# A gated recurrence with a gated causal convolution: one hand-ordered plan exchanged for another, with two chunks' input products moved to GpSimd

## The chip, the cores and the metric

The kernel runs on one core of a Trainium2 chip. Times are device microseconds (us) of one execution; the time of a kernel is the median of several executions. The core has five engines that work side by side and wait for each other through semaphores: TensorE (PE; its weight loads are shown as PEld), VectorE (DVE), ScalarE (ACT), GpSimd (POOL) and SyncE (SP), which here only issues transfers. A letter q behind an engine's name (ACTq, SPq) is its queue as the issuer of a DMA.

## The reference

The inputs x, r_gate and i_gate are 4 x 6336 x 256 in fp32, that is 25,344 tokens of 256 channels. A linear recurrence runs over the tokens of each of the four sequences, and a gated unit with a causal convolution of five taps follows.

```python
a_base = sigmoid(a_param)
a_t    = exp(8.0 * sigmoid(r_gate) * log(clip(a_base, 1e-6, 1 - 1e-6)))
x_g    = sqrt(max(1 - a_t * a_t, 1e-6)) * sigmoid(i_gate) * x
h      = a_t[:, t] * h + x_g[:, t]          # for each t; y[:, t] = h
gate   = sigmoid(sum over k of conv_w[k] * y[t - 4 + k])
out    = (gate * (y @ w_val)) @ w_out
```

## The kernel before

The tokens are cut into 27 chunks (CHUNKS): one of 512, 23 of 1024, then 512, 512 and 256. Work on the output side is cut further into parts of 512 tokens (a chunk c has parts c.0 and c.1), and the 256 channels are two halves h of 128. Inputs come token-major (tokens on the partitions); the scan needs channels on the partitions, so TensorE transposes in between.

The order of all work is written out by hand in a string, PLAN (lines 33 to 118). Each word is an operation with its chunk, its half or part, and the PSUM bank that it writes (-1 for none). The loop at line 466 runs through the words and calls the function of that name, so each engine's queue holds its operations in the plan's order, and an engine that waits holds up all that is behind it. The operations, in the order in which a chunk passes through them:

| word | engine, line | what it does |
|---|---|---|
| ldri, ldx | SP, L220, L224 | load r_gate and i_gate of a chunk, and its x; 1 MB each for 1024 tokens |
| tanh | ACT, L290 | tanh of half of both gates (sigmoid from tanh), to bf16 in place |
| srT, exp | PE L295, ACT L304 | transpose the r gate, then a_t = exp(...) into aring |
| e | POOL, L310 | a_t squared into ering |
| s1, u | POOL, L318, L345 | i gate + 1, then times x: uring |
| xc, ux | PE L327, DVE L335 | for chunks in X_PE, in place of s1 and u: x is copied into PSUM by an identity matmul, two 128-token blocks at a time, and VectorE makes (gate + 1) times x from there |
| sq | ACT, L354 | square root of 1 - a_t squared, for up to three chunks at once; needs another activation table, so a table load (L472) before and after |
| nT, xg | PE L367, DVE L374 | transpose the root back, multiply it into uring |
| xgT, scan | PE L382, DVE L395 | transpose the gated input, then the recurrence of one half |
| conv, tg | PE L407, ACT L417 | convolution of a part as matmuls with diagonal weights, then tanh |
| val, gv | PE L425, DVE L430 | y @ w_val, then the gating product |
| out, osbD or osbA | PE L439, DVE L454 or ACT L450 | the last product, and its copy from PSUM to one of five output buffers |
| store | ACTq, L459 | the output buffer to HBM; 512 KB |

So u.12 is the product of chunk 12, scan.3.1 the recurrence of the second half of chunk 3, store.8.0 the store of the first part of chunk 8.

Buffers set how far the engines may run apart: three for the gates (NRI), two for x (NX), five for aring and ering, four for uring, three for yring, five for the output (NOSB). ldx.c therefore waits for u.(c-2), the i gate of ldri.c for u.(c-3), and its r gate for srT.(c-3). Output parts are numbered through, and the copy of a part waits until the store of the part five before it has landed.

All DMAs, loads and stores together, signal their landing on eight semaphores, taken in turn in the plan's order. In the built program a DMA waits, before it is issued, for the one eight places ahead of it in that order, wherever this is not already certain. A store waits in ScalarE's queue, a load in SyncE's.

Of the kernel before, what the change touches and what calls it, by code (L numbers as in the profile page):

```python
# [16 lines left out]
X_PE = [0, 1]  # L17
# [16 lines left out]
ldri.0.-1 ldri.1.-1 ldx.0.-1 ldx.1.-1 ldri.2.-1 ldw.-1 tanh.0.-1 srT.0.0.7 srT.0.1.5 exp.0.1.-1 exp.0.0.-1 e.0.0.-1  # L34
tanh.1.-1 e.0.1.-1 xc.0.1.0 xc.0.0.6 ux.0.0.-1 xc.1.2.1 u.0.-1 sq.0.1.-1 ux.1.2.-1 srT.1.0.0 ldri.3.-1 xc.1.1.5
ldx.2.-1 nT.0.0.7 srT.1.1.4 exp.1.0.-1 xg.0.0.-1 ux.1.1.-1 exp.1.1.-1 xc.1.0.0 tanh.2.-1 xc.1.3.5 e.1.1.-1 ux.1.0.-1
e.1.0.-1 wc.-1 srT.2.0.3 s1.2.-1 srT.2.1.2 xgT.0.0.4 exp.2.0.-1 scan.0.0.-1 exp.2.1.-1 e.2.0.-1 u.1.-1 tanh.3.-1
ldx.3.-1 ldri.4.-1 e.2.1.-1 u.2.-1 srT.3.1.3 srT.3.0.6 xgT.0.1.1 sq.1.2.-1 s1.3.-1 ldx.4.-1 ldri.5.-1 nT.2.0.7
nT.2.1.0 u.3.-1 xg.2.0.-1 exp.3.1.-1 xg.2.1.-1 nT.1.1.7 scan.0.1.-1 nT.1.0.5 tanh.4.-1 xg.1.1.-1 conv.0.0.0 xg.1.0.-1
xgT.2.0.3 e.3.1.-1 ldx.5.-1 xgT.1.1.4 ldri.6.-1 xgT.1.0.2 scan.1.1.-1 tg.0.0.-1 exp.3.0.-1 s1.4.-1 srT.4.1.1  # L40
exp.4.1.-1 scan.1.0.-1 val.0.0.4 e.3.0.-1 tanh.5.-1 srT.4.0.6 gv.0.0.-1 conv.1.0.0 u.4.-1 scan.2.0.-1 xgT.2.1.7
tg.1.0.-1 srT.5.1.5 srT.5.0.4 exp.4.0.-1 scan.2.1.-1 val.1.0.0 exp.5.1.-1 e.4.1.-1 ldx.6.-1 ldri.7.-1 exp.5.0.-1
gv.1.0.-1 conv.2.0.6 tanh.6.-1 e.5.1.-1 out.0.0.4 conv.1.1.0 osbD.0.0.-1 e.4.0.-1 val.2.0.2 tg.1.1.-1 val.1.1.4
e.5.0.-1 store.0.0.-1 tg.2.0.-1 out.1.0.0 conv.2.1.6 osbD.1.0.-1 s1.5.-1 sq.3.3.-1 gv.1.1.-1 u.5.-1 gv.2.0.-1
out.2.0.0 out.1.1.4 osbD.2.0.-1 osbD.1.1.-1 s1.6.-1 nT.3.1.3 ldri.8.-1 nT.3.0.2 ldx.7.-1 val.2.1.0 tg.2.1.-1 xg.3.0.-1
# [95 lines left out]
def kernel(  # L141
# [54 lines left out]
    with tc.manual_schedule():  # L196
# [310 lines left out]
```

## Time and profile before

| | us |
|---|---|
| median of three runs | 310.66 (309.64, 310.66, 311.12) |
| the profiled execution | 311.12 |
| its span in the profile | 309.0 |
| busy: ScalarE, VectorE, TensorE, GpSimd | 278.5, 252.3, 248.1, 235.2 |
| L310 e, 54 times, on GpSimd | 93.6 |
| L345 u, 25 times, on GpSimd | 96.0 |
| L395 scan, 52 of 54 in this group, on VectorE | 113.4 |
| L290 tanh, 27 times, on ScalarE | 90.2 |
| table loads L472, 22, on ScalarE | 28.2 |
| DMA: 104.74 MB, mean over the span | 339 GB/s |

A line of an engine's timeline has the start in us, the busy us of the instructions merged in it, engine, source line, operation, what it writes and reads with shapes, and in brackets the idle time before it with what ended that. The chain of waits is followed back from the last instruction: start, us, and what the time was spent on. The table of stretches gives busy times of all engines for a window of the span.

### The profile page before, as it was taken

The page shows a single profiled execution, that of the slowest core. Times are in us where ns is not written, and L with a number is a line of the kernel's source. Part 1 is how long each engine was busy: PE and PEld are TensorE (multiplying, and loading weights), DVE is VectorE, ACT ScalarE, POOL GpSimd, SP SyncE. Part 2 cuts the span into 40 slices and gives each one's busy share as a digit, 9 for nine tenths or more (in the row PEclk, how much of TensorE's full clock was granted, in tenths as well). Part 3 has the DMA queues.
Part 4 walks back from the last instruction along what each step waited for, and adds up shares of the span by engine and source line. Part 5 has one row for each costly group of instructions (what it writes and reads, how often), then busy time and mean ns, then how long its engine had stood idle before and what let it go on. Part 6 is the DMA issues. An engine that isn't in the chain of part 4 may idle for free.

```text
span 309.0 us, 6335 instructions
## 1 busy us (share of the span) xinstructions
PE 248.1 (80%) x2627; PEld 167.7 (54%) x2627; DVE 252.3 (82%) x208; ACT 278.5 (90%) x185; POOL 235.2 (76%) x118
## 2 busy tenths in 40 slices
PE   0582577958888898799489998988899987999994
PEld 0232454447546564557257665675666655565763
DVE  1052079479898989999499999999999998989893
ACT  6799999999999999998699999999999979868632
POOL 3229998997998999899996799989959993038000
PEclk9995589999999999999979999999999999999999
DMA  7999999998997999999999997999897764182555
GB/s 288 427 360 422 382 417 364 365 352 318 389 377 263 413 414 422 421 421 421 428 423 365 363 390 280 376 426 424 336 369 309 285 249 137 69 337 109 200 212 237
DMA packets 19466, 104.74 MB, mean 339 GB/s; under 512 B 2151, under 2 KB 2670, under 8 KB 10606
## 3 DMA queue, kind: packets, MB, share of 16 engines
q1 hardware_dynamic: 12224, 78.39, 65.0%
q10 hardware_dynamic: 7214, 25.96, 21.0%
q8 instruction: 20, 0.33, 0.4%
q14 instruction: 8, 0.07, 0.1%
HBM read 78.39 MB, written 25.95 MB: 338 GB/s over the span
## 4 chain that ended last, share of the span: by engine, by line
PE 24%; DMA 21%; POOL 18%; ACT 17%; issue 11%; DVE 6%; ACTq 1%; SPq 1%; POOLq 0%; DVEq 0%
DMA gate<-in_i_gate_dram 13%; POOL uring L345 10%; PE pp L407 7%; PE pp L439 6%; DMA xr<-in_x_dram 6%; ACT gate L290 5%; POOL ering L310 5%; ACT tgr L417 4%; PE pp L425 4%; ACT aring L304 4%; POOL gate L318 3%; PE pp L367 3%; DMA out_dram<-osb 3%; DVE yring L395 3%; PE pp L327 2%
## 5 line engine op out<-in xcount | busy, mean ns | idle before, releaser
L310 POOL TENSOR_TENSOR ering<-aring 128x1024 f32<-128x1024 f32 (+2 forms) x54 | 93.6, 1754 | 36.7 <-ACT aring L304 35.1
L395 DVE TENSOR_TENSOR_SCAN yring<-aring,yring,pp 128x1024 bf16<-128x1024 f32 (+2 forms) x52 | 113.4, 2193 | 4.1 <-PE pp L382 4.1
L345 POOL TENSOR_TENSOR uring<-gate,xr 128x2048 bf16<-128x2048 bf16 (+2 forms) x25 | 96.0, 3845 | 4.3 <-PE pp L382 2.6
L290 ACT ACTIVATE gate<-gate 128x4096 bf16<-128x4096 f32 (+2 forms) x27 | 90.2, 3340 | 7.6 <-DMA xr<-in_x_dram 3.9
L407 PE MATMUL pp<-yring,diag 64*64 64x512 bf16 (+13 forms) x1224 | 65.3, 341 | 5.2 <-DVE yring L395 2.2
L430 DVE SCALAR_TENSOR_TENSOR gvr<-tgr,pp 128x1024 bf16<-128x1024 bf16 (+1 forms) x50 | 59.4, 1200 | 8.9 <-ACT tgr L417 6.7
L439 PE MATMUL pp<-wo,gvr 128*128 128x256 bf16 x396 | 52.7, 279 | 13.9 <-DVE gvr L430 7.9
L304 ACT ACTIVATE aring<-pp,khf 128x1024 f32<-128x1024 bf16 (+2 forms) x54 | 59.3, 1144 | 3.9 <-PE pp L295 2.2
L417 ACT ACTIVATE tgr<-pp 128x1024 bf16<-128x1024 f32 (+1 forms) x50 | 50.5, 1024 | 10.0 <-PE pp L407 8.6
L439 PEld LDWEIGHTS <-gvr 128*128 128x128 bf16 x396 | 42.5, 115 | 23.8 <-DVE gvr L430 11.1
L425 PE MATMUL pp<-yring,wv 128*128 128x512 bf16 (+1 forms) x200 | 50.5, 377 | 6.1 <-DVE osb L454 2.2
L454 DVE COPY osb<-pp 128x1024 f32<-128x1024 f32 x41 | 49.0, 1211 | 6.1 <-PE pp L439 5.9
L318 POOL TENSOR_SCALAR gate<-gate 128x2048 bf16<-128x2048 bf16 (+2 forms) x25 | 44.5, 1781 | 5.4 <-ACT gate L290 5.4
L407 PEld LDWEIGHTS <-diag 64*64 64x64 bf16 x1224 | 30.6, 107 | 30.6 <-issue 14.5
L354 ACT ACTIVATE ering<-ering,b 128x4096 bf16<-128x4096 f32 (+4 forms) x16 | 46.4, 2932 | 0.1
L374 DVE TENSOR_TENSOR uring<-uring,pp 128x1024 bf16<-128x1024 bf16 (+1 forms) x50 | 32.0, 672 | 12.7 <-PE pp L367 12.5
L295 PE MATMUL pp<-ident_b,gate 128*128 128x128 bf16 x396 | 31.4, 229 | 13.2 <-ACT gate L290 11.1
L295 PEld LDWEIGHTS <-gate 128*128 128x128 bf16 x396 | 26.6, 103 | 21.9 <-ACT gate L290 14.0
L367 PE MATMUL pp<-ident_f,ering 128*128 128x128 f32 x198 | 32.3, 303 | 5.4 <-ACT ering L354 3.9
L382 PE MATMUL pp<-ident_f,uring 128*128 128x128 f32 x198 | 31.5, 282 | 6.1 <-ACT tgr L417 2.8
L367 PEld LDWEIGHTS pp<-ident_f,ering 128*128 128x128 f32 x198 | 27.8, 208 | 11.6 <-ACT ering L354 4.8
L425 PEld LDWEIGHTS <-wv 128*128 128x128 bf16 x200 | 18.8, 98 | 23.9 <-issue 11.1
(33 smaller groups left out, 86.9 us busy)
## 6 DMA issues: line engine op xcount, KB each, us to landing
out_dram<-osb ACTq DMA_DIRECT2D x49, 512.0 KB, 7.9
gate<-in_r_gate_dram SPq DMA_DIRECT2D x23, 1024.0 KB, 11.7
gate<-in_i_gate_dram SPq DMA_DIRECT2D x23, 1024.0 KB, 9.6
xr<-in_x_dram SPq DMA_DIRECT2D x23, 1024.0 KB, 10.0
gate<-in_r_gate_dram SPq DMA_DIRECT2D x3, 512.0 KB, 7.7
gate<-in_i_gate_dram SPq DMA_DIRECT2D x3, 512.0 KB, 10.7
xr<-in_x_dram SPq DMA_DIRECT2D x3, 512.0 KB, 3.4
yring<-in_moe_w_val_dram SPq DMA_DIRECT2D x1, 256.0 KB
```

Of the source, the lines that this page charges most:

```text
L290: nc.scalar.activation(out=tgate[:, s0:s0 + 2, 0:w], in_=gate[:, s0:s0 + 2, 0:w], func=ACT.Tanh, scale=0.5)
L295: nc.tensor.transpose(out=ppb[:, bank * 2 * BANK + j * P:bank * 2 * BANK + (j + 1) * P], in_=tgate[:, slot(c, 0), j * D + h * P:j * D + (h ...
L304: nc.scalar.activation(out=dst, in_=src, func=ACT.Exp, scale=khf[:, h:h + 1], bias=khf[:, h:h + 1])
L310: nc.gpsimd.tensor_tensor(out=ering[:, c % NE, h * n:(h + 1) * n], in0=a, in1=a, op=ALU.mult)
L345: nc.gpsimd.tensor_tensor(out=u, in0=t, in1=xt, op=ALU.mult)
L367: nc.tensor.transpose(out=pp[:, d0:d0 + P], in_=src[:, w, :], identity=ident_f[:])
L395: nc.vector.tensor_tensor_scan(out=yring[:, h, y0:y0 + n], data0=aring[:, c % NA, h, 0:n], data1=src, initial=prev, op0=ALU.mult, op1=ALU.add)
L407: nc.tensor.matmul(out=pp[col * HP:(col + 1) * HP, b0 + d0:b0 + d1], lhsT=diag[r * HP:(r + 1) * HP, h, kk, :], rhs=yring[r * HP:(r + 1) * ...
L417: nc.scalar.activation(out=tgr[:, nth[k] % NTG, :, 0:n], in_=two(live["conv", k], n), func=ACT.Tanh, scale=0.5)
L425: nc.tensor.matmul(out=pp[:, (bank + m) * BANK:(bank + m) * BANK + n], lhsT=wv[:, hk, m, :], rhs=yring[:, hk, y0:y0 + n], start=(hk == 0), ...
L430: nc.vector.scalar_tensor_tensor(out=gvr[:, nth[k] % NGV, :, 0:n], in0=tgr[:, nth[k] % NTG, :, 0:n], scalar=1.0, in1=two(live["val", k], n ...
L439: nc.tensor.matmul(out=pp[:, bank * BANK + j * D:bank * BANK + (j + 1) * D], lhsT=gvr[:, nth[k] % NGV, m, 0:n].rearrange("c (p q) -> c q p ...
```

## The change

X_PE, the list of chunks whose gated input is made by TensorE and VectorE, becomes empty: chunks 0 and 1 take s1 and u on GpSimd like all others, and six xc and their ux words leave the plan. The rest is a new PLAN: the same operations in another order and with other PSUM banks (868 words in place of 876). Twelve evictions at the end are osbA in place of nine: 22.0, 22.1, 23.1 and 24.0 move from VectorE to ScalarE and 26.0 moves to VectorE. No function changes. Stores stay on ScalarE's queue, the buffer counts stay, and the weight casts (wc) stay on ScalarE.

The core of the diff, with the plan's lines that the text speaks of:

```diff
-X_PE = [0, 1]
+X_PE = []
...
-ldri.0.-1 ldri.1.-1 ldx.0.-1 ldx.1.-1 ldri.2.-1 ldw.-1 tanh.0.-1 srT.0.0.7 srT.0.1.5 exp.0.1.-1 exp.0.0.-1 e.0.0.-1
-tanh.1.-1 e.0.1.-1 xc.0.1.0 xc.0.0.6 ux.0.0.-1 xc.1.2.1 u.0.-1 sq.0.1.-1 ux.1.2.-1 srT.1.0.0 ldri.3.-1 xc.1.1.5
-ldx.2.-1 nT.0.0.7 srT.1.1.4 exp.1.0.-1 xg.0.0.-1 ux.1.1.-1 exp.1.1.-1 xc.1.0.0 tanh.2.-1 xc.1.3.5 e.1.1.-1 ux.1.0.-1
...
-val.3.1.4 exp.8.1.-1 gv.3.1.-1 e.6.0.-1 conv.4.1.6 ldx.9.-1 exp.8.0.-1 ldri.10.-1 xgT.5.0.3 store.2.0.-1 tg.4.1.-1
...
-xg.11.0.-1 store.5.0.-1 tg.7.1.-1 xgT.9.1.0 e.12.0.-1 scan.9.1.-1 exp.12.1.-1 out.7.0.2 tanh.13.-1 val.7.1.4 u.12.-1
...
-ldri.16.-1 tg.9.0.-1 nT.11.1.7 val.9.0.4 e.13.0.-1 store.8.0.-1 tanh.15.-1 gv.8.1.-1 conv.9.1.0 gv.9.0.-1 e.14.1.-1
...
-store.14.0.-1 exp.21.0.-1 gv.16.0.-1 nT.19.0.6 xgT.18.0.7 store.15.0.-1 tanh.22.-1 xg.20.0.-1 out.15.1.4 xg.19.0.-1
...
-val.22.0.4 u.25.-1 xg.24.0.-1 conv.22.1.6 sq.25.2.-1 gv.22.0.-1 xgT.24.1.3 conv.23.1.0 scan.24.1.-1 xgT.24.0.5
...
+ldri.0.-1 ldri.1.-1 ldx.0.-1 ldx.1.-1 ldri.2.-1 ldw.-1 tanh.0.-1 srT.0.0.2 exp.0.0.-1 e.0.0.-1 srT.0.1.2 exp.0.1.-1
+s1.0.-1 tanh.1.-1 e.0.1.-1 u.0.-1 ldri.3.-1 srT.1.0.2 s1.1.-1 srT.1.1.0 ldx.2.-1 sq.0.1.-1 u.1.-1 nT.0.0.4 xg.0.0.-1
...
+val.0.0.4 exp.3.0.-1 gv.0.0.-1 sq.1.2.-1 s1.3.-1 ldx.4.-1 ldri.5.-1 e.3.0.-1 nT.1.1.0 nT.2.0.6 u.3.-1 srT.3.1.5
...
+xg.3.1.-1 xg.4.0.-1 xgT.3.0.5 scan.3.0.-1 store.1.0.-1 exp.6.0.-1 srT.7.0.7 srT.7.1.4 exp.7.0.-1 xgT.3.1.6 s1.7.-1
...
+srT.8.1.7 s1.8.-1 ldx.9.-1 val.3.1.4 exp.8.1.-1 ldx.8.-1 gv.3.0.-1 ldri.10.-1 out.2.1.0 e.7.0.-1 tanh.9.-1 conv.4.0.2
...
+scan.5.1.-1 out.3.0.2 store.3.1.-1 store.2.1.-1 exp.9.1.-1 xgT.5.0.5 e.8.0.-1 val.4.0.6 store.2.0.-1 gv.4.0.-1 u.8.-1
...
+s1.12.-1 ldri.14.-1 nT.10.0.1 tg.7.0.-1 ldx.13.-1 xg.10.0.-1 exp.12.1.-1 conv.7.1.4 xg.9.1.-1 u.12.-1 gv.7.0.-1
...
+ldx.15.-1 tg.9.0.-1 e.13.1.-1 gv.8.1.-1 xgT.11.1.4 store.8.0.-1 store.7.1.-1 tanh.15.-1 val.9.0.2 scan.11.1.-1
...
+tg.16.1.-1 xg.20.1.-1 srT.22.0.2 xgT.18.0.3 s1.22.-1 osbD.16.0.-1 store.14.0.-1 store.15.0.-1 exp.22.0.-1 srT.22.1.5
...
+xgT.19.1.4 scan.18.1.-1 ldri.24.-1 out.16.1.0 exp.21.1.-1 srT.23.0.3 osbD.16.1.-1 store.15.1.-1 tg.17.0.-1 srT.23.1.5
...
+tg.20.1.-1 out.19.1.2 e.26.1.-1 e.26.0.-1 nT.24.0.1 conv.21.0.4 xg.24.0.-1 sq.25.2.-1 gv.20.0.-1 val.20.1.0
+osbA.19.1.-1 out.20.0.6 gv.20.1.-1 store.18.0.-1 store.19.1.-1 xgT.22.1.2 store.19.0.-1 osbA.20.0.-1 nT.23.1.0 u.26.-1
...
```

ScalarE's queue around the places that move, as the two plans give it:

```
before  ... tg.9.0 store.8.0 tanh.15 tg.9.1 store.8.1 sq.12.3 ...
after   ... tg.9.0 store.8.0 store.7.1 tanh.15 tg.9.1 sq.12.3 store.9.0 store.8.1 ...
before  ... tanh.25 tg.19.0 sq.23.2 osbA.19.0 tg.19.1 exp.25.1 tanh.26 ... exp.25.0 exp.26.0 ... tg.22.0 sq.25.2 ...
after   ... tanh.25 tg.19.0 exp.25.0 exp.25.1 sq.23.2 osbA.19.0 tg.19.1 tanh.26 ... tg.20.1 sq.25.2 osbA.19.1 ...
```

and GpSimd's:

```
before  ... u.11 s1.12 e.12.0 u.12 s1.13 e.12.1 u.13 ...
after   ... u.11 s1.12 u.12 e.12.1 s1.13 e.12.0 u.13 ...
```

## The prediction

> **What bounds the kernel now.** I read the page's busy times first, then the table of stretches, then the waits inside the stretches that stand out, then the chain.
>
> ```profile
> PE 248.1 (80%) x2627; PEld 167.7 (54%) x2627; DVE 252.3 (82%) x208; ACT 278.5 (90%) x185; POOL 235.2 (76%) x118
> ```
>
> ScalarE has most work, but the shares hide the stages. Columns here: stretch, its length, then busy us (and instructions) of PE, weight loads, VectorE, ScalarE and GpSimd, the granted TensorE clock, the DMA share, GB/s.
>
> ```profile
> 0.00:20.00 20.00, 9.70 (x40) 5.46 (x41) 3.73 (x11) 14.92 (x13) 4.36 (x10) 1.00 0.92 362
> 20.00:40.00 20.00, 9.91 (x55) 7.10 (x54) 5.41 (x8) 19.94 (x13) 18.49 (x8) 0.61 1.01 391
> ...
> 100.00:146.00 46.00, 39.43 (x462) 27.58 (x461) 44.26 (x34) 45.36 (x29) 44.30 (x21) 1.00 1.01 417
> 146.00:150.00 4.00, 3.58 (x35) 1.71 (x33) 3.54 (x5) 0.23 (x1) 4.00 (x3) 1.00 1.03 430
> 150.00:160.00 10.00, 5.62 (x28) 3.63 (x29) 6.18 (x5) 9.97 (x4) 9.83 (x5) 0.83 1.02 425
> 160.00:246.00 86.00, 78.52 (x885) 54.59 (x884) 84.95 (x68) 85.67 (x56) 76.41 (x35) 1.00 0.92 359
> 246.00:265.00 19.00, 15.23 (x158) 10.75 (x157) 18.06 (x14) 17.34 (x12) 11.66 (x6) 1.00 0.58 204
> 265.00:309.00 44.00, 38.92 (x464) 24.91 (x463) 36.08 (x32) 26.18 (x29) 10.19 (x9) 0.99 0.48 192
> ```
>
> From 20 us to 246 us ScalarE hardly rests, VectorE joins it from 100 us, and after 265 us TensorE works off what is left. So a change gains only at the start, at 146 to 154 us, or in the tail. The middle hole, in time order (ScalarE's timeline, the last line VectorE's):
>
> ```profile
> 144.80 1.07 ACT L417 ACTIVATE tgr<-pp 128x1024 bf16<-128x1024 f32 x1
> 149.31 0.34 ACTq L459 DMA_DIRECT2D out_dram<-osb  x1
> 149.78 3.62 ACT L290 ACTIVATE gate<-gate 128x4096 bf16<-128x4096 f32 x1 [3.90 <-DMA xr<-in_x_dram]
> ...
> 154.34 1.22 DVE L430 SCALAR_TENSOR_TENSOR gvr<-tgr,pp 128x1024 bf16<-128x1024 bf16 x1 [3.77 <-ACT tgr L417]
> ```
>
> ScalarE stands still 3.90 us, not for its gates but behind store.8.0, which by the turn of the eight DMA semaphores waits for ldx.14. That load was issued at 136.43, after u.12, and took 12.8 us: landed 149.2, store at 149.31. VectorE then waits 3.77.
>
> In the tail GpSimd waits 17.49 us and the loads come in two late lumps:
>
> ```profile
> 227.84 11.40 DMA gate<-in_i_gate_dram
> ...
> 243.98 10.73 DMA gate<-in_i_gate_dram
> ```
>
> **The start, 0 to 68 us.** Removed: 12 fp32 matmuls at L327 (8.8 us) and six products at L335 (4.2 us, with 11.1 us of idle VectorE before them). Added on GpSimd, from the rows of L318 and L345 by size: s1.0 1.05, s1.1 1.90, u.0 2.16, u.1 4.12, together 9.2 us.
>
> ```profile
> 15.83 1.34 DVE L335 SCALAR_TENSOR_TENSOR uring<-gate,pp 128x512 bf16<-128x512 bf16 x2 [10.69 <-PE pp L327]
> ...
> 21.20 3.74 POOL L310 TENSOR_TENSOR ering<-aring 128x1024 f32<-128x1024 f32 x2 [8.85 <-ACT aring L304]
> ```
>
> The cover of the 9.2 us is GpSimd's wait of 8.85 us, and 3.76 us before the first e. Step by step: e.0.0, s1.0, e.0.1 end at 12.3; u.0 (x landed 11.9) at 14.5; tanh.1 is done at 14.33, so s1.1 ends at 16.4, u.1 at 20.5. exp.1.1, no longer behind six L327 matmuls, ends at 20.4 (now 21.1), so the pair e.1 ends at 24.2 (now 24.9), s1.2 and e.2 at 30.1 (now 30.8). Without that cover e.1 would be 9.2 us late, and sq.1.2 behind it. The lead of 0.7 us is spent: sq.1.2 stands behind tg.0.0 and exp.3.0 (0.95 + 1.10), so it ends at 38.0 instead of 36.6, and scan.1.1, behind four xg and srT.4.1, starts at 46.3 against 43.34. But ScalarE reaches the end of tanh.6 at 58.8 (now 57.95) with one tg more done (0.95), and VectorE reaches xg.3.0 at 68.4 (now 67.09) with one gv more done (1.13). Both are level: 0, between -1 (0.7 kept) and +2 (the late scan not made up).
>
> The granted clock was 0.61 in 20 to 40 us already, and 16 transposes of L367 took 3.96 us there. In the Trainium skill, "TensorE: Matmul & The Clock Gate", section "What's actually happening", an idle window of about 3.4 us halves the clock, which speaks against taking PE work from the first 18 us. By it nT.0.0 would grow by an estimated half microsecond; by the row, and as ScalarE is the bound there, nothing.
>
> **68 to 160 us.** New costs: scan.3.1 now has srT.7.0 and srT.7.1 ahead of its transpose on TensorE, and they need tanh.7 (ends 73.5): VectorE loses 1.8 us. It is covered by the 3.1 us that VectorE idles between 97.5 and 149 us (1.01, 0.27, 0.17, 0.68, 0.29, 0.20, 0.46). The gain: on GpSimd e.6.1 moves ahead of u.6, into the wait for tanh.7, so that only s1.7 and e.6.0 stand before u.7 where s1.7, e.6.1 and e.7.0 stand today: u.7 ends at 81.4 (now 82.9), and the lead stays near 2 us to u.11 (124.5, now 126.5). Then u.12 follows s1.12 at once, where e.12.0 (1.90 and 1.48 of waiting) stood between: 124.5 + 1.9 + 4.1 = 130.5 against 135.95. ldx.14 is issued with it at 131 and, at the 12.8 us of today's row, lands at 143.7. The store that waits for it is now store.7.1, after tg.9.0, at about 144.9. So the stall goes. I take -3.5; the ends are -4.3 (3.90 and the 0.45 us before exp.11.1, the like of it behind store.4.0) and 0, since DMA ran at 417 to 430 GB/s here and may not deliver earlier what is asked earlier.
>
> **160 to 246 us.** At sq.21.2 the two plans have issued the same ScalarE set; ScalarE rests 0.3 us and VectorE 1.0 of 86, so nothing is to gain. A loss: store.14.0 moves behind tg.16.1, and osbD.16.1 needs its buffer again after only 5.7 us of VectorE work. Stores landed in 2.6 / 4.4 / 7.8 us (least, median, most) in 220 to 246 us, so VectorE waits 0 to 2.1 us; gv and scans queue behind it. With like misfits I take +1.0, ends 0 and +3. The Trainium skill, "DMA: Bandwidth & Descriptors", section "Anatomy of one DMA", gives about 2.0 us and bytes over 436 GB/s, an estimated 3.2 us for 512 KB: no wait at all, and a sum 1 us lower. The rows, with loads in flight, are the ones I follow.
>
> **The tail.** Four evictions of 1024 columns go from VectorE (1.13 each by their spacing) to ScalarE (1.0) and osb.26.0 goes back (0.65): VectorE -3.9, ScalarE +3.4, where ScalarE is busy only 26 of the last 44 us. ldx.23 no longer stands behind ldx.24, u.22 has two e fewer ahead, so gates 25 are asked for near 238 instead of 243.98 and the 1.56 us wait of tanh.25 goes. exp.25, exp.26 and sq.25.2 with two table loads (4.3 us, done at 286.7 now) come ahead of osbA.19.1 and end at 273.7. What stands behind them is tg.21: tg.21.0 at 275.7 instead of 271.78. TensorE is covered by val.20.1, out.20.0, xgT.22.1, nT.23.1 and nT.26.0 (0.87 + 0.93 + 0.45 + 0.47 + 0.24 = 3.0 us); were these gone, the tail would lose 3. Followed through by the same rows, scan.21.1 ends at 264.1 (now 265.1), scan.22.1 at 276.7 (the last scan.22 now 276.2), tg.23.1 at 289.9, the last out at 302.7 (now 305.4): -2.7, less 0.7 for three stores in a row (0.34 each) ahead of osbA.20.0: -2.0, ends -3 and +1.
>
> **Sum.** 0 - 3.5 + 1.0 - 2.0 = -4.5. The profiled execution took 311.12 us (its span of 309.0 and 2.1 around it), which gives 306.6; it lies 0.46 above the median of the runs, 310.66, so against that: **306.2 us**.
>
> **Rivals.** *Slower: a load stuck behind another.* ldx.9 now stands ahead of ldx.8 on SyncE's queue and waits for u.7; ldx.8 is issued at 81.9, today at 73.35. The x loads of 72 to 84 us took 6.4 and 12.6 us, so it lands between 88.3 and 94.5. Two things wait for it: u.8 (GpSimd free at 90.7) and, by the semaphore's turn, store.2.0 on ScalarE's queue (90.8), with sq.6.3 and all that follows behind it. At 94.5 both lose 3.8 us, GpSimd's lead is gone, and the stall on ldx.14 is back: 311.1 + 3.8 + 1.0 - 2.0 - 0.46 = 313.4. It makes the kernel slower from a landing at about 93.3 on, with the middle's gain lost. For it: the 12.6 us row. Against: little else is in flight at 82 us, since SyncE's queue held everything back. 0.22.
>
> *No change: the DMA is the bound in 100 to 150 us.* The share is 1.01; then ldx.14 lands when its bytes come, and the 3.5 us remain: 0 + 0 + 1.0 - 2.0 = -1.0, 309.7. Against it: 164 GB/s in 96 to 100 us, so bytes were left to ask for earlier. 0.16.
>
> *The tail does not gain, the middle does:* -3.5 + 1.0 = -2.5, 308.2; it counts as faster. With the forecast, 0.62.
>
> **How the numbers follow.** Measurements of this kernel tell 0.5% (1.55 us) from no change: faster is below 309.1, slower above 312.2. Faster 0.62, same 0.16, slower 0.22. All lower ends (-8.3) give 302.4, all upper ones (+6) 316.7; I leave a tenth out on each side: 302.8 to 313.4. The forecast's own range is 302.8 to 309.1.
>
> **What would show it.** No wait of 3 us of ScalarE near 145; a GpSimd wait before u.8, or a long one of ScalarE before the square roots of chunks 6 to 8, is the slower rival; a VectorE wait at an eviction of chunk 16 is the buffer; TensorE idle near 270 to 276 us is the tail's risk. Wrong it would be above all if a store elsewhere on ScalarE's queue meets a load that is not yet there: every store does so by its turn.

## The result, and the profile after

The changed kernel took 313.67 us, the median of 4 runs (313.18 to 314.63); the kernel before took 310.59 beside it. The ratio is 1.0106, 95% interval 1.0072 to 1.0141: slower by 1.1%, some 3.3 us (2.2 to 4.4), where 306.2 was predicted. The profiled execution is at the median (span 311.9 us). Here and below medians are of all runs, while ratios leave out a run that is more than 1.5% above the fastest of its kernel.

The page of the changed kernel, busy times, to be held against those of before:

```profile
PE 247.2 (79%) x2615; PEld 167.4 (54%) x2615; DVE 244.8 (79%) x199; ACT 281.7 (90%) x188; POOL 244.1 (78%) x122
```

The work moved as the diff says: VectorE has 7.5 us less, GpSimd 8.9 more, ScalarE 3.2 more (the evictions of the tail). No engine became a new bound by its sum. The same stretches as before (columns: stretch, length, busy us of PE, weight loads, VectorE, ScalarE, GpSimd, TensorE clock, DMA share, GB/s):

```profile
0.00:20.00 20.00, 5.51 (x33) 3.88 (x33) 1.82 (x8) 15.22 (x13) 12.55 (x14) 1.00 0.91 362
20.00:40.00 20.00, 8.85 (x58) 5.24 (x59) 3.55 (x3) 19.94 (x14) 19.76 (x10) 0.79 1.02 401
...
146.00:150.00 4.00, 3.46 (x36) 2.12 (x37) 4.00 (x4) 1.86 (x2) 4.00 (x3) 1.00 1.01 425
...
160.00:246.00 86.00, 75.32 (x846) 51.69 (x843) 81.85 (x65) 82.75 (x52) 77.21 (x36) 1.00 0.96 376
246.00:265.00 19.00, 18.29 (x177) 12.43 (x176) 18.05 (x16) 18.52 (x15) 17.52 (x11) 0.91 0.33 127
265.00:309.00 44.00, 40.00 (x469) 25.65 (x467) 34.74 (x29) 29.86 (x32) 4.19 (x5) 0.99 0.48 193
```

The hole at 146 to 150 us is smaller (ScalarE busy 1.86 of 4, before 0.23). But from 160 to 246 us both leading engines lost some 3 us: VectorE 81.85 where it had 84.95, ScalarE 82.75 where it had 85.67. The two places, first the middle: the timeline of ScalarE, and the load's piece from the chain of waits.

```profile
145.47 1.08 ACT L416 ACTIVATE tgr<-pp 128x1024 bf16<-128x1024 f32 x1
148.24 0.34 ACTq L458 DMA_DIRECT2D out_dram<-osb  x1
148.70 3.62 ACT L289 ACTIVATE gate<-gate 128x4096 bf16<-128x4096 f32 x1 [2.14 <-DMA xr<-in_x_dram]
...
132.84 15.32 DMA xr<-in_x_dram
```

ldx.14 is asked for at 132.84, which is 3.6 us earlier than before, but it takes 15.32 us and not 12.8, so it lands at 148.16, hardly sooner. store.7.1 goes out at 148.24, and ScalarE has stood 2.14 us. Then the late place, from the timeline of all engines:

```profile
222.43 5.99 SPq L223 DMA_DIRECT2D xr<-in_x_dram  x2
233.82 0.62 PE L294 MATMUL pp<-ident_b,gate 128*128 128x128 bf16 x8
234.51 0.33 SPq L219 DMA_DIRECT2D gate<-in_r_gate_dram  x1
242.78 1.91 ACT L289 ACTIVATE gate<-gate 128x2048 bf16<-128x2048 f32 x1 [2.15 <-DMA gate<-in_i_gate_dram]
244.78 1.04 POOL L317 TENSOR_SCALAR gate<-gate 128x1024 bf16<-128x1024 bf16 x1 [3.27 <-ACT gate L289]
245.63 1.22 DVE L429 SCALAR_TENSOR_TENSOR gvr<-tgr,pp 128x1024 bf16<-128x1024 bf16 x1 [2.10 <-ACT tgr L416]
```

The r gates of chunk 24 go into the buffer that srT.21.1 reads. The new order puts srT.21.1 behind the transposes of chunk 22, at 233.82, and the load follows it at once, at 234.51. Three engines wait for it in a row.

### The profile page after: what moved, and what is told of

Same layout as the page of the kernel before. It is cut to its first block, busy times and chain, and to the rows that moved or that the text cites. A ratio compares the mean times of both kernels' runs of the same rounds, so it can differ in the third digit from the quotient of the medians.

```text
span 311.9 us, 6317 instructions
## 1 busy us (share of the span) xinstructions
PE 247.2 (79%) x2615; PEld 167.4 (54%) x2615; DVE 244.8 (79%) x199; ACT 281.7 (90%) x188; POOL 244.1 (78%) x122
## 4 chain that ended last, share of the span: by engine, by line
PE 28%; DVE 16%; ACT 15%; DMA 10%; issue 9%; POOL 2%; ACTq 1%; SPq 0%; DVEq 0%; POOLq 0%
PE pp L406 8%; PE pp L438 7%; PE pp L424 6%; DVE gvr L429 6%; DMA gate<-in_i_gate_dram 6%; DMA xr<-in_x_dram 5%; DVE yring L394 5%; ACT tgr L416 4%; ACT ering L353 3%; ACT aring L303 3%; DVE osb L453 3%; PE pp L366 3%; ACT gate L289 3%; DVE uring L373 3%; PE pp L381 2%
## 5 line engine op out<-in xcount | busy, mean ns | idle before, releaser
L344 POOL TENSOR_TENSOR uring<-gate,xr 128x2048 bf16<-128x2048 bf16 (+2 forms) x27 | 102.3, 3790 | 8.3 <-issue 4.1
L406 PE MATMUL pp<-yring,diag 64*64 64x512 bf16 (+14 forms) x1224 | 64.7, 343 | 4.5 <-ACT tgr L416 1.3
L438 PE MATMUL pp<-wo,gvr 128*128 128x256 bf16 x396 | 53.6, 281 | 10.0 <-DVE gvr L429 6.4
L317 POOL TENSOR_SCALAR gate<-gate 128x2048 bf16<-128x2048 bf16 (+2 forms) x27 | 47.4, 1755 | 13.6 <-ACT gate L289 12.3
L424 PE MATMUL pp<-yring,wv 128*128 128x512 bf16 (+1 forms) x200 | 54.5, 397 | 3.8 <-ACT tgr L416 1.9
L294 PE MATMUL pp<-ident_b,gate 128*128 128x128 bf16 x396 | 33.2, 233 | 22.0 <-ACT gate L289 14.7
L453 DVE COPY osb<-pp 128x1024 f32<-128x1024 f32 (+1 forms) x38 | 44.9, 1200 | 5.5 <-PE pp L438 4.6
L381 PE MATMUL pp<-ident_f,uring 128*128 128x128 f32 x198 | 32.6, 288 | 7.8 <-ACT aring L303 2.3
L424 PEld LDWEIGHTS <-wv 128*128 128x128 bf16 x200 | 19.7, 102 | 22.5 <-issue 11.1
## 6 DMA issues: line engine op xcount, KB each, us to landing
gate<-in_r_gate_dram SPq DMA_DIRECT2D x23, 1024.0 KB, 12.8
```

The source lines that it names most:

```text
L294: nc.tensor.transpose(out=ppb[:, bank * 2 * BANK + j * P:bank * 2 * BANK + (j + 1) * P], in_=tgate[:, slot(c, 0), j * D + h * P:j * D + (h ...
L344: nc.gpsimd.tensor_tensor(out=u, in0=t, in1=xt, op=ALU.mult)
L406: nc.tensor.matmul(out=pp[col * HP:(col + 1) * HP, b0 + d0:b0 + d1], lhsT=diag[r * HP:(r + 1) * HP, h, kk, :], rhs=yring[r * HP:(r + 1) * ...
L424: nc.tensor.matmul(out=pp[:, (bank + m) * BANK:(bank + m) * BANK + n], lhsT=wv[:, hk, m, :], rhs=yring[:, hk, y0:y0 + n], start=(hk == 0), ...
L438: nc.tensor.matmul(out=pp[:, bank * BANK + j * D:bank * BANK + (j + 1) * D], lhsT=gvr[:, nth[k] % NGV, m, 0:n].rearrange("c (p q) -> c q p ...
```

## The experiments

Each edit is made in the order's words; `-1` stands for no PSUM bank. Ratios are to the kernel before, run beside it on the same chip (medians of 310.06 to 310.37).

**One part of the change alone.** gpsimd_inputs_only:

```diff
-X_PE = [0, 1]      (and the words xc.* and ux.*, u.0, u.1 in their places)
+X_PE = []          e.0.0 s1.0 tanh.1 e.0.1 u.0 s1.1 u.1 ...
```

> The kernel of before with one part of the change: X_PE = [], so s1 and u of chunks 0 and 1 on GpSimd stand where the matmuls and products of L327 and L335 were; all else in the order of before. If GpSimd's work hides in its wait for ScalarE (8.85 us) and the later start comes from the new order: 310.4 us, 309.6 to 311.2, with VectorE's xg.3 at 67 us as before. If the part itself costs (e.1 and u.2 late on GpSimd, or a lower clock of TensorE): 312 us and above, with VectorE late at 67 us.

Measured: 310.11 us, ratio 1.0003 (0.9987 to 1.0019); xg.3 started at 68.03. The 9.2 us of GpSimd work hide in its wait, as predicted, and ScalarE's table load ahead of sq.6.3 came at 89.77, within the 88.87 to 90.36 of the five profiles with the start of before (before, late_only, tail_only, before_store80_behind_tanh15, before_two_moves). So the loss comes from the order.

**One stretch of the order alone.** The orders of the two kernels are spliced: one up to a cut, then all that is left in the sequence of the other. A few PSUM banks were changed where the splice needed it (nT.4.1 and nT.5.1; five words in the tail; xgT.14.0). start_only cuts behind tanh.7, late_only behind sq.12.3, tail_only behind sq.21.2; middle_only takes the changed order only between tanh.7 and sq.15.3.

> The changed kernel's order up to the scaled tanh of chunk 7 (about 71 us, all gated inputs of chunks 0 and 1 on GpSimd), then everything that is left in the order of before. If the start costs nothing that lasts (ScalarE reached tanh.7 0.7 us behind its like, VectorE xg.3.0 some 3.5 us behind, and the 3.9 us stall of ScalarE at 146 us of before swallows both): 310.6 us, 309.9 to 311.3. If the start is where the 3 us went: 312.5 to 314.

Measured: 313.2 us, ratio 1.0098 (1.0066 to 1.0130). The start alone costs.

> The order of before, X_PE = [0, 1] with it, up to the square roots of chunks 12 to 14 (about 154 us), then the rest in the changed order. If the loss lies behind 160 us (the late gates of chunk 24 at 235 to 243 us, and a tail that gains little) and the stretch before gained 1.1 us: 314.7 us, 313.9 to 315.5. If the loss lies in the start or the middle: 309.5 to 311.

Measured: 314.4 us, ratio 1.0123 (1.0097 to 1.0149). So does the rest behind 154 us.

> The order of before up to the square roots of chunks 21 and 22 (about 246 us), then the rest in the changed order (sq.25.2 early, more evictions on ScalarE). If the tail gained the 0.5 us that the two traces show between sq.21.2 and the last eviction: 310.1 us, 309.5 to 310.8. If it gains the 2 us of the prediction once nothing is late in front of it: 308.6 us. If the tail loses: above 311.3.

Measured: 311.22 us, ratio 1.0030 (1.0012 to 1.0049). The tail neither gains 2 us nor 0.5: by the ratio it loses 0.9 (0.4 to 1.5). The two profiles do not show where: from the table load ahead of sq.21.2 to the start of the last eviction it took 59.50 us (244.99 to 304.49), and 59.56 in the kernel before (245.90 to 305.46).

> The order of before up to tanh.7 (about 69 us), then the changed order up to the square roots of chunks 15 to 17 (about 184 us), then what is left in the order of before. If the start alone costs some 3 us and the stretch behind it gains 4 that the changed kernel spent on making up for it: 306.4 us (305.4 to 307.6). If the middle gains only the 1.1 us by which the changed kernel is ahead at 184 us, since DMA delivers ldx.14 no earlier: 309.3 us.

Measured: 315.69 us, ratio 1.0177 (1.0148 to 1.0205). This run says little of the middle: at its two seams it has holes that neither kernel has (VectorE 4.66 us at 74 us; ScalarE 3.58 and 2.45 us at 196 and 201 us).

**The stall at 146 us.** In each kernel one word is moved, the store that waits for ldx.14. The turn of the semaphores goes by the order of the transfers in the built program, which is not quite the order of the words: counted in the words, the eighth transfer ahead of store.8.0 is the i gate load of chunk 15; in the built program it is ldx.14. The partners named here and below are read from the built programs. The two moves leave all partners as they are.

```diff
 changed kernel:  ... store.8.0 -store.7.1 tanh.15 +store.7.1 val.9.0 ...
 kernel before:   ... e.13.0 -store.8.0 tanh.15 +store.8.0 gv.8.1 ...
```

> The changed kernel with store.7.1 moved behind tanh.15 on ScalarE's queue, so that the scaled tanh of chunk 15 no longer stands behind the store that waits for ldx.14. If only the store's turn held ScalarE: tanh.15 starts at about 146.6 in place of 148.70, and the time falls by up to 2.1 us to 311.6 (311.2 to 312.6). If the gates of chunk 15, or what follows them, come no sooner because the transfers are saturated: the wait comes back at tanh.15 itself or at the next load, and the time stays at 313 to 314.5.

> The kernel of before with one word moved: store.8.0 behind tanh.15, which is all that ScalarE's 3.90 us at 146 us waits for there. If the turn of the store alone holds ScalarE: tanh.15 starts at 146 to 147 in place of 149.78 and the time is 307.3 us (306.3 to 308.4), faster than both kernels. If the saturated transfers set the pace behind it: 309.5 to 310.8, with the wait moved to tanh.15's gates or to a later load.

Measured: 311.8 us (ratio 1.0048, 1.0025 to 1.0071) for the changed kernel, and 308.01 us (0.9941, 0.9916 to 0.9966) for the kernel before, which beats both. ScalarE's timeline, first of the changed kernel with its word moved, then of the kernel before with its own:

```profile
145.79 3.68 ACT L289 ACTIVATE gate<-gate 128x4096 bf16<-128x4096 f32 x1
147.78 0.34 ACTq L458 DMA_DIRECT2D out_dram<-osb  x1
```

```profile
144.35 3.69 ACT L290 ACTIVATE gate<-gate 128x4096 bf16<-128x4096 f32 x1
147.94 0.34 ACTq L459 DMA_DIRECT2D out_dram<-osb  x1
```

tanh.15 has no bracket of idle time any more; the store still goes out when ldx.14 lands, but nothing stands behind it. The two starts of tanh.15 also show ScalarE 1.4 us later in the changed order once nothing holds it; in both_mends (below), which has the same order up to there, tanh.15 starts at 147.25, so it is 1.4 to 2.9 us.

**Loads asked for earlier.** x_loads_in_order puts each x load ahead of its successor:

```diff
-... u.4 exp.4.1 ... ldx.6 scan.2.1 srT.5.1 ldx.5       -ldx.9 ... ldx.8      -ldx.21 ldx.20
+... s1.4 ldx.5 ldri.6 ... ldx.6                        +ldri.9 ldx.8 ... ldx.9   +ldri.21 ldx.20 ... ldx.21
```

> The changed kernel with three loads back in their natural order on SyncE's queue: ldx.5 ahead of ldri.6, ldx.8 behind ldri.9, ldx.20 behind ldri.21 (in the changed kernel each stands behind the next chunk's x load, which waits for a later u). In every run so far ldx.14 landed when 56.4 to 57.1 MB had been moved, whenever it was issued. The changed kernel has two holes in the DMA share, 0.39 in 48 to 52 us and 0.31 in 80 to 84, some 5 us of transfer time together. If the transfers as such bound the kernel up to 150 us: the holes close, ldx.14 lands near 144.5 after the same 56.5 MB, ScalarE's wait before tanh.15 goes, and the time is 311.6 us (310.6 to 312.5), gates24 still late. If landing has another cause: tanh.15 starts at 148 to 149 as before and the time is 313 to 314.5.

Measured: 316.52 us, ratio 1.0222 (1.0184 to 1.0259), the opposite of what was expected. The stretches of the changed kernel, then of this one:

```profile
48.00:52.00 4.00, 2.72 (x35) 2.20 (x36) 3.91 (x3) 4.00 (x4) 4.00 (x2) 0.90 0.39 164
80.00:84.00 4.00, 4.00 (x74) 2.49 (x67) 4.00 (x3) 4.00 (x4) 4.00 (x2) 1.00 0.31 118
104.00:108.00 4.00, 3.70 (x42) 3.34 (x41) 4.00 (x3) 4.00 (x4) 2.99 (x2) 1.00 0.98 357
```

```profile
48.00:52.00 4.00, 2.95 (x34) 2.32 (x36) 3.91 (x3) 4.00 (x4) 4.00 (x2) 0.83 0.92 383
80.00:84.00 4.00, 3.95 (x76) 2.50 (x70) 4.00 (x3) 3.96 (x4) 4.00 (x2) 1.00 0.91 325
104.00:108.00 4.00, 3.59 (x40) 3.31 (x42) 4.00 (x3) 4.00 (x4) 3.08 (x2) 1.00 0.71 187
```

The holes at 48 and 80 us closed, and a new one opened at 104 us: what had come early was not followed by more, since the next loads wait for buffers that compute frees. From 108 us on both ran at a share of 1.02, and tanh.15 started at 148.76, at the old time. The loss lies elsewhere, at 202 us (SyncE's queue and ScalarE):

```profile
194.90 0.33 SPq L219 DMA_DIRECT2D gate<-in_r_gate_dram  x1
...
201.92 2.32 ACT L303 ACTIVATE aring<-pp,khf 128x1024 f32<-128x1024 bf16 x2
...
207.57 0.34 ACTq L458 DMA_DIRECT2D out_dram<-osb  x1
208.01 3.62 ACT L289 ACTIVATE gate<-gate 128x4096 bf16<-128x4096 f32 x1 [3.78 <-DVE gvr L429]
```

The store at 207.57 is store.13.0. In the compiled program of this run it waits, by the turn of its semaphore, for the r gates of chunk 21 (issued 194.90, 12.6 us to landing); in the changed kernel it waits for store.11.0. Moving ldx.20 shifted the turns. The profile names VectorE, but the eviction had ended at 201.4.

> As x_loads_in_order, but with ldx.20 left where the changed kernel has it. In x_loads_in_order ScalarE stood 3.78 us before tanh.20, behind store.13.0, whose semaphore had its turn after the r gates of chunk 21, issued at 194.9; in the changed kernel its turn is after store.11.0. If that turn alone made it slower: no such wait here, ldx.14 lands at 148.2 as before (the loads that closed the holes at 48 and 80 us leave a hole at 104 instead), and the time is that of the changed kernel, 313.6 us (312.8 to 314.5). If the earlier loads themselves cost: 315 to 317.

Measured: 314.62 us (312.06 to 318.75), ratio 1.0102 (1.0055 to 1.0149). The wait before tanh.20 is gone, tanh.15 starts at 148.86. The time is that of the changed kernel within a wide spread, so the extra loss of x_loads_in_order went with the move of ldx.20 and the new turn that came with it.

**The late stretch.**

```diff
 gates24_early:       srT.21.0 +srT.21.1 ... exp.21.0 +exp.21.1 ...  (out of their places behind u.22)
 gates24_free_store:  as above, and  -store.16.1 exp.23.1 ldx.24 ... exp.23.0 +store.16.1
 late_three_moves:    as above, and  +store.14.0 tg.16.1 ... osbD.16.0 -store.14.0
```

srT.21.1 also writes bank 4 in place of 5 in these three, and the turns of the stores behind 225 us shift.

> The changed kernel with two words of the order moved: srT.21.1 behind srT.21.0 and exp.21.1 behind exp.21.0, so that the r gates of chunk 24, whose buffer srT.21.1 reads, can be asked for at about 228.5 us in place of 234.51. If that late load is what stops ScalarE for 2.15, VectorE for 3.05 and GpSimd for 3.27 us at 242 to 248 us, and these are on the path: 311.3 us (310.8 to 312.1) and no wait on the gates of chunk 24. If the tail is held by something else (TensorE): 313 to 313.7, with the wait gone. If the load waits for something else (ldx.23 ahead of it): wait and time stay.

Measured: 316.88 us (312.65 to 317.38), ratio 1.0151 (1.0100 to 1.0201). That is later than either expectation with the wait gone, and widely spread. The gates' wait is gone, and another is there (ScalarE's and VectorE's timeline of this run):

```profile
241.50 1.23 DVE L453 COPY osb<-pp 128x1024 f32<-128x1024 f32 x1 [1.10 <-PE pp L424]
...
242.76 0.34 ACTq L458 DMA_DIRECT2D out_dram<-osb  x1
243.15 1.20 ACT L303 ACTIVATE aring<-pp,khf 128x1024 f32<-128x1024 bf16 x1 [2.72 <-DVE osb L453]
```

ScalarE now comes to store.16.1 before VectorE has done its eviction, and exp.23.1 stands behind the store.

> As gates24_early, and store.16.1 moved behind exp.23.0 on ScalarE's queue. In gates24_early the wait for the gates of chunk 24 was gone, but ScalarE stood 2.72 us at 243 us, in front of exp.23.1, behind store.16.1, whose eviction VectorE had not done. If that store is what took the gain back: 311.3 us (310.6 to 312.3), no ScalarE wait over 1 us in 225 to 250 us. If something else moved it (the eviction itself late, its buffer not yet stored): 314 to 317 as there.

Measured: 314.54 us, ratio 1.0146 (1.0107 to 1.0185). That wait went too, and the next came up on VectorE's timeline, the output buffer that the prediction had named:

```profile
240.91 1.22 DVE L453 COPY osb<-pp 128x1024 f32<-128x1024 f32 x1 [1.36 <-DMA out_dram<-osb]
```

> The changed kernel with the stretch of 225 to 248 us mended in three places: srT.21.1 and exp.21.1 early (gates of chunk 24 in time), store.16.1 behind exp.23.0 (ScalarE does not stand behind an eviction), store.14.0 ahead of tg.16.1 as in the order of before (the output buffer that osbD.16.1 needs). From tanh.15 to osbA.20.0 the changed kernel took 127.29 us with 122.48 of ScalarE busy; the kernel with the order of before up to 246 us took 124.51 with 122.35. If the three waits together are that difference: 311.2 us (310.4 to 312.2) and 125 us between the two. If the order there only moves its waits about: 313 to 315, 127 us.

Measured: 312.63 us (311.1 to 314.94), ratio 1.0092 (1.0064 to 1.0121), 125.28 us from tanh.15 to osbA.20.0 in its profile (273.94 less 148.66). The stretch is as short as expected, 2.0 us less than in the changed kernel; the median fell by 1.0 only, less than its spread, and the ratios (1.0106, 1.0092) do not tell the two apart. Nor did the first moves alone shorten the stretch: it took 129.83 us in gates24_early and 127.23 in gates24_free_store, against 127.29. So it took the buffer's wait gone as well, and that the three waits are the cost of this stretch is seen in one profile, not shown by the time.

both_mends has these three moves, and store.7.1 behind tanh.15 as well:

> The changed kernel with store.7.1 behind tanh.15 and with the three moves of late_three_moves. Alone they gave -1.9 and -1.0 us. If they add: 310.8 us (310.0 to 311.6), which leaves against the mended kernel of before (308.0) some 2.8 us for the start and the tail. If the earlier end of the one is eaten by the other's wait: 311.6 to 312.6.

Measured: 311.24 us, ratio 1.0023 (0.9998 to 1.0048): 2.6 us below the changed kernel by the ratios. By the ratios the two gave 1.8 and 0.4 alone, so they add within the intervals.

**The start.** In the changed kernel TensorE stops inside out.1.0, since that tile is two banks wide (6 and 7) and srT.6.1 had been given bank 7. TensorE and VectorE of the changed kernel, then VectorE of the one with the other bank:

```diff
-srT.6.1.7
+srT.6.1.5
```

> The changed kernel with one digit of the order changed: srT.6.1 writes bank 5 of PSUM in place of bank 7. In the changed kernel out.1.0 fills banks 6 and 7, and TensorE stops for 1.86 us in the middle of its eight matmuls (60.84 to 62.70 us) until exp.6.1 has read bank 7; osbD.1.0 on VectorE waits 3.93 us behind that and xg.3.0 starts at 71.88. If that is a step of the late start: the pause is gone, osbD.1.0 waits about 2.0, xg.3.0 starts near 70, and the time is 312.4 us (311.6 to 313.1), since the run with the changed start alone kept VectorE's lateness to the end. If the wait of ScalarE for ldx.14 at 148 us takes up whatever VectorE gains: 313.3 to 314.

```profile
62.70 1.01 PE L438 MATMUL pp<-wo,gvr 128*128 128x256 bf16 x4 [1.86 <-ACT aring L303]
63.82 1.23 DVE L453 COPY osb<-pp 128x1024 f32<-128x1024 f32 x1 [3.93 <-PE pp L438]
```

```profile
60.99 1.23 DVE L453 COPY osb<-pp 128x1024 f32<-128x1024 f32 x1 [1.57 <-PE pp L438]
...
76.87 2.35 DVE L394 TENSOR_TENSOR_SCAN yring<-aring,yring,pp 128x1024 bf16<-128x1024 f32 x1 [3.03 <-PE pp L381]
```

Measured: 315.0 us, ratio 1.0172 (1.0134 to 1.0211). The pause went, and VectorE gave the gain back at 76.87, where scan.3.1 waits behind srT.7.0 and srT.7.1: the scan ended at 79.2, where it ended at 78.9. Why the time rose by 1.3 us is not explained by anything at the start.

start_mended is store71_behind_tanh15 with that bank, and xgT.3.1 ahead of srT.7.0:

> store71_behind_tanh15 with srT.6.1 in bank 5 (as in other_bank) and xgT.3.1 ahead of srT.7.0 and srT.7.1 on TensorE, so that neither out.1.0 nor scan.3.1 holds VectorE. VectorE's scan.3.1 should then end near 76 us in place of 78.6. If VectorE's lateness is the cost of the start: tanh.15 starts near 144.5 in place of 145.79 and the time is 310.3 us (309.5 to 311.2). If ScalarE's own lateness at tanh.5 and tanh.7 (gates of chunk 5, 1.6 us) sets it: 311.3 to 312.5, tanh.15 at 145.5 to 146.

Measured: 311.19 us, ratio 1.0041 (1.0018 to 1.0064), against 1.0048 without it: no difference. The two waits went, but xg.3.0 then waited 3.12 us for its transposes, which need ScalarE's square roots, and scan.3.1 ended at 78.5, as late as without the edit; tanh.15 started at 147.38, later than either expectation (the profiled run, 314.42 us, is the slowest of the twelve). So VectorE's two waits are not what sets its lateness: ScalarE's square roots stand behind them.

start_only_free_store is start_only with store.8.0 behind tanh.15 (and nT.4.1 and nT.5.1 in banks 3 and 5 in place of 5 and 3), to be held against before_store80_behind_tanh15, which has the same order from tanh.7 on:

> start_only (the changed order up to tanh.7, then the order of before) with store.8.0 behind tanh.15. If the new start costs what start_only showed, by VectorE and ScalarE coming late and not by the load at 146 us: tanh.15 starts some 3 us later than the 144.35 of before_store80_behind_tanh15, and the time is 310.7 us (309.9 to 311.6). If the cost in start_only came by way of ldx.14 and the store that waits for it: 308 to 309.

Measured: 311.2 us, ratio 1.0026 (1.0002 to 1.0050), against 0.9941: the new start costs 0.85%, 2.6 us, with the load at 146 us out of the way. The stretch of 40 to 60 us, first of before_store80_behind_tanh15, then of this run:

```profile
40.00:60.00 20.00, 15.87 (x181) 9.67 (x186) 13.71 (x10) 19.40 (x13) 19.13 (x10) 0.94 0.97 391
```

```profile
40.00:60.00 20.00, 15.44 (x186) 11.47 (x184) 15.13 (x11) 18.30 (x11) 17.41 (x9) 0.89 0.86 332
```

ScalarE and GpSimd have 1.1 and 1.7 us less work done there, and DMA moved less. ScalarE's table load ahead of sq.6.3 comes at 91.34 where it came at 89.14, and tanh.15 at 146.86 where it came at 144.35: the 2.5 us are never made up in that order. The waits of ScalarE say where they come from, first of before_store80_behind_tanh15 again, then of this run:

```profile
45.76 3.62 ACT L290 ACTIVATE gate<-gate 128x4096 bf16<-128x4096 f32 x1 [0.16 <-DMA gate<-in_i_gate_dram]
```

```profile
45.33 3.62 ACT L289 ACTIVATE gate<-gate 128x4096 bf16<-128x4096 f32 x1 [1.08 <-DMA gate<-in_i_gate_dram]
```

This is tanh.5, which starts when its gates have landed, nearly at the same time in both; but in the new start ScalarE has one exp (1.2 us) less behind it by then. From 18 us to sq.6.3 ScalarE's waits add up to 2.49 us here and to 0.48 there: 1.08 and 0.16 for these gates, the rest for TensorE.

**The tail.** tail_less_conv leaves three of the five taps of the convolution out in chunks 22 to 26:

```diff
-            for kk in reversed(range(CONV_K)):
+            for kk in (reversed(range(CONV_K)) if c < 22 else (CONV_K - 1, 0)):
```

> The changed kernel with three of the five taps of the convolution left out in chunks 22 to 26 (so its results differ there): 84 matmuls, about 5 us of TensorE at 1.27 us for 20 of them, nearly all of it after 276 us. If TensorE bounds the tail, so that evictions moved from VectorE to ScalarE could not shorten it: 309 us (308.2 to 310.2). If ScalarE's order there (sq.25.2 and exp.26 ahead of tg.21) or VectorE bounds it: 312.5 to 313.7.

Measured: 311.91 us, ratio 1.0066 (1.0032 to 1.0100). The tail of the changed kernel, then of this one:

```profile
280.00:290.00 10.00, 9.96 (x105) 6.37 (x104) 9.62 (x7) 5.30 (x6) 0.00 (x0) 1.00 0.19 75
290.00:300.00 10.00, 10.00 (x129) 6.22 (x131) 9.37 (x10) 6.06 (x6) 0.00 (x0) 1.00 0.62 245
```

```profile
280.00:290.00 10.00, 8.37 (x70) 5.16 (x69) 9.89 (x9) 6.10 (x7) 0.00 (x0) 1.00 0.14 54
290.00:300.00 10.00, 9.56 (x88) 5.55 (x88) 8.44 (x10) 6.90 (x7) 0.00 (x0) 1.00 0.68 272
```

From osbA.20.0 to the last eviction's start it took 29.63 us in place of 30.94, so some 5 us of TensorE work were worth 1.3 (1.2 by the ratios). Neither expectation holds: TensorE is full (19.96 of 20 us), but VectorE is right behind it (19.00 of 20), so taking work from one alone gives little. In the kernel before TensorE was just as full there (20.00 of 20 us, VectorE 18.98).

**A last try on the faster kernel.** before_two_moves is before_store80_behind_tanh15 with ldx.23 ahead of ldx.24.

> before_store80_behind_tanh15 with ldx.23 ahead of ldx.24 on SyncE's queue, as in the changed order, so that ldx.23 does not stand behind a load that waits for u.22. If the 1.10 us that ScalarE waits for the gates of chunk 25 at 251 us shrinks with it: 307.2 us (306.5 to 308.0). If that wait comes from elsewhere or the new turns of the stores cost: 308 to 310.

Measured: 312.15 us, ratio 1.0057 (1.0035 to 1.0079): some 4 us lost by moving one load (3.6 by the ratios). The queues of this run:

```profile
222.13 0.33 SPq L220 DMA_DIRECT2D gate<-in_i_gate_dram  x1
...
228.93 0.34 ACTq L459 DMA_DIRECT2D out_dram<-osb  x1
229.31 3.62 ACT L290 ACTIVATE gate<-gate 128x4096 bf16<-128x4096 f32 x1 [3.44 <-DMA gate<-in_i_gate_dram]
```

The store is store.15.0. In the compiled program it now waits for the i gates of chunk 23 (issued 222.13); without the move it waited for the r gates of chunk 23. One shift of the turns, and ScalarE stands 3.44 us. What the move of ldx.23 itself costs beside the turn was not separated.

## Why the prediction was wrong

| stretch | predicted | measured | from |
|---|---|---|---|
| inputs on GpSimd | 0 | 0.1 | gpsimd_inputs_only, ratio 1.0003 |
| start, order | 0 (-1 to +2) | +2.6 | 1.0026 less 0.9941, of 310 us |
| 68 to 160 us | -3.5 (-4.3 to 0) | -2.5 | tanh.15 (below), less the start |
| 160 to 246 us (measured to osbA.20.0) | +1.0 (0 to +3) | +2.8 | 127.29 less 124.51 us from tanh.15 to osbA.20.0, changed kernel and tail_only |
| tail | -2.0 (-3 to +1) | +0.9 | tail_only, ratio 1.0030 |
| sum | -4.5 | +3.8 | measured in all +3.3 (2.2 to 4.4) |

The 0.1 of the first row is part of the 2.6 below it and is not added again. The rows of the start and of 68 to 160 us are one measured sum, +0.1 at tanh.15, split by what the start cost where no store held ScalarE; while tanh.15 waits for ldx.14, that wait takes up part of a late start. The next two rows have a check: late_only, with the changed order behind 154 us alone, lost 3.8 us (1.0123), against 2.8 and 0.9.

**Right:** that ScalarE at 146 us stands behind a store that waits for ldx.14, and that this is on the path. Two runs show it, with 1.8 and 1.8 us by the ratios. Right too that GpSimd's added work is free, in the order of before, and that the wait for the gates of chunk 25 goes.

**Start.** The step that failed is "Both are level". tanh.6 ended at 59.7, not 58.8, and xg.3.0 started at 71.88, not 68.4. I had not seen that out.1.0 covers the bank of srT.6.1. But that is not where the time went: I had asked only whether VectorE and ScalarE were level at one point each, and ScalarE, which hardly rests behind it, was 2.2 us late by sq.6.3 (91.34 and 89.14). By the traces ScalarE is late for two reasons. Less of its work stands ahead of tanh.5, whose gates come no sooner: in the thirteen profiles with the changed start it waited 1.08 to 3.16 us for them, in the five with the start of before 0 to 1.03. And it has more short waits for TensorE, 1.41 against 0.32 us in the pair above. No run took these waits away, so this is read and not shown. Three other causes are ruled out. VectorE's two waits are not it (start_mended). The hole in the transfers at 48 us is not it: with the hole closed the table load ahead of sq.6.3 came at 92.29 (loads_5_8_in_order) and 92.16, where the changed kernel had 92.27. TensorE's clock is not it: in gates24_early it was 1.00 from 20 to 68 us, and the table load came at 93.14.

**Middle.** The step that failed is "at the 12.8 us of today's row, lands at 143.7". u.12 ended at 132.4, two us later than the 130.5 that I had worked out, since the lead of 2 us that GpSimd was to keep to u.11 was not there (u.11 ended at 126.36, before at 126.46), but still 3.5 earlier than before; ldx.14 was asked for at 132.84 and took 15.32 us. The rival "the DMA is the bound in 100 to 150 us" was right on this step, and I gave it 0.16. So a row's time from issue to landing is here mostly what is already queued: at 423 GB/s (108 to 148 us) the 15.32 us are some 6.5 MB, and the load itself is 1 MB. The Trainium skill, "DMA: Bandwidth & Descriptors", section "Anatomy of one DMA — SWDGE (gpsimd) path", has 2.0 us and the bytes at 436 GB/s, an estimated 4.4 us for such a load; the section gives this for transfers that GpSimd issues, and the loads and stores here go out from SyncE and ScalarE, those of the prediction's 3.2 us too. The x loads of 108 to 148 us took 7.9 to 15.3 us in the two kernels. So the wait fell from 3.90 to 2.14 us and no further. Start and middle together gave nothing: tanh.15 started at 149.02 us on average in three profiles with the order of before up to there (before, late_only, tail_only) and at 149.11 in five with the changed one (after, gates24_early, gates24_free_store, late_three_moves, tail_less_conv).

**160 to 246 us.** The step that failed is "with like misfits I take +1.0": the price was a guess within its range, and the misfit was another one. osbD.16.1 did not wait in the changed kernel; what ScalarE, VectorE and GpSimd waited for were the late gates of chunk 24, by srT.21.1. I had checked where loads stand on SyncE's queue, but not when the TensorE instruction that frees a load's buffer comes. The buffer wait that I had named was hidden behind it, and showed with 1.36 us once the gates came in time; only with both gone did the stretch shrink, to 125.28 us.

**Tail.** The step that failed is the -2.0 itself. I had counted what VectorE sheds and followed single instructions with TensorE as cover, but TensorE is full there from 280 us on, as it was before. That tg.21.0 came at 279.29, not 275.7, is mostly the lateness of the stretches ahead: in tail_only it came at 276.68. (The 0.7 us for three stores at 0.34 should have been 1.0.) What VectorE and ScalarE trade among themselves (ScalarE 11.36 of 20 us busy in 280 to 300) then shortens nothing. Why the tail lost 0.9 us by the ratio, and did not merely stay as it was, is open.

**The slower rival** (ldx.9 stuck ahead of ldx.8) did not happen as put: u.8 started at 91.87 and store.2.0 at 91.07 without a long wait. The hole in the transfers at 80 to 84 us is its trace, and closing it was worth nothing (loads_5_8_in_order, 1.0102 against 1.0106). The kernel is slower by the sum of three stretches, a case that none of the rivals described.

**What to carry over.** First, where stores go out on an engine that also computes, and semaphores are handed out in turn, list for each store which transfer its semaphore waits for, from the built program, and do it again after every edit, also for edits far away: here one word moved was worth -1.8 us in each kernel, and one word, by a new turn, went with a stall of 3.78 or 3.44 us and some 3 or 4 us of time. Second, price a load that is asked for earlier by the queue ahead of it, not by its old time to landing. Third, in an order tuned by hand a stretch is to be judged by when ScalarE, VectorE and TensorE all reach its end; a wait taken away uncovers the next one behind it.

## What the runs showed of the hardware that was not expected

A store's semaphore wait stops the arithmetic behind it on the same engine: 3.90, 2.14, 3.78 and 3.44 us of ScalarE in four kernels, and none in the two where only the store was moved. The Trainium skill, "DMA: Bandwidth & Descriptors", section "Anatomy of one DMA — SWDGE (gpsimd) path", says that a wait for a semaphore happens on the issuing sequencer, before the transfer is dispatched, not on the DMA engines; the traces agree, the store going out at 207.57 and the waiting instruction starting at 208.01.

The granted clock in 20 to 40 us does not follow the order: 0.61 in the kernel before, 1.00 in gpsimd_inputs_only with less TensorE work there, and 0.79 and 1.00 in two runs of the very same start (after, gates24_early). In shorter stretches it was 1.00 or 0.50: 0.50 from 26 to 40 us in the kernel before, 1.00 from 20 to 30 and 0.50 from 32 to 40 us in the changed one, 1.00 throughout in gates24_early. So the half clock that the prediction weighed against the change did come, but later than before and not at nT.0.0 (1.00 in 16 to 20 us); and the run without it was no earlier at sq.6.3 (93.14, against 92.27).

A tile that is two banks wide can stop in its middle: out.1.0 ran four of its eight matmuls, paused 1.86 us for the reader of the second bank, and ran the other four; with srT.6.1 in another bank (other_bank) the eight ran without a pause.
